# Half of the last batch's first product as seven block products, and two sums of w_in moved to GpSimd

## The chip, the cores and the metric

The kernel runs on one core of one Trainium2 chip. The metric is the device time in microseconds (us) of one execution; a run's time is the median of several executions. The engines are named as the profile names them: PE (TensorE: matmuls, with PEld for its weight loads), DVE (VectorE), ACT (ScalarE), POOL (GpSimd) and SP (SyncE, which here only issues DMAs). SBUF is the on-chip memory of all engines; PSUM holds the eight banks that PE writes its products to.

## What is computed

```python
scores  = scale * x @ state^T            # per batch (8) and head (8): 512 x 32, depth 64
xread   = softmax(scores) @ state        # 512 x 64
sread   = softmax(scale * state @ x^T) @ x   # 32 x 64
rows    = concat(xread, sread) per batch, heads side by side   # 8 x 544 rows of 512
h       = rows @ w_in                    # w_in 512 x 2048
g       = maximum(0.01 * h, h)           # leaky rectifier
out     = g @ w_out                      # w_out 2048 x 512, fp32
```

Two products of the feed-forward part make nearly all of the arithmetic. Operands are bf16, sums fp32.

## The kernel before

The kernel goes batch by batch through 512 token rows (`xread`); the 256 `sread` rows of all batches go through the feed-forward part together at the end.

For a batch, `xread @ w_in` is never formed from `xread`: `a.M` (256 x 2048, bf16, as [128, 2, 2048]) is state times w_in of that batch, made by `a_m` and copied out by `m_evict`, and `a.aT` (256 x 512, as [128, 2, 512]) holds the softmax weights. So **the first product** of a batch is `M^T aT`, depth 256 = two groups `g` of 128. `ff1(a, hT, j)` (L369) makes 128 of the 2048 rows of h: two matmuls of 512 columns into a PSUM tile `ph` (two buffers, used in turn), then the rectifier on ACT (L377) into `hT[:, j, :]`. The loop over `s` from 0 to 15 calls it with `j = s`.

**The second product** of a batch (`Batch`, `Fast`, L525 and L575) is done with seven block products where eight are usual. Its operands are A (from `hT`, split in two by token and two by depth) and B (from w_out). The products 1, 2, 6, 5, 7, 3, 4 accumulate in two PSUM banks `yq`: 1, 6, 7 and 4 in the first, 2, 5 and 3 in the second. Four sums of A, `su0` to `su3` (`sums`, L546, DVE, in halves: m 0 to 3 needs `hT` 0 to 7, m 4 to 7 the rest), and four of B (`tw`, made once) are the operands of products 6, 5, 7, 3 and 4. ACT saves the banks after 1, 6, 5 and 7 (L566), DVE joins them with the later ones (L569) into `yo`, and POOL adds one pair (L627).

A "unit" is one product at one m: two matmuls of 256 columns (L557). A batch has 56 units. 15 of them, of products 1 and 2, run in the batch's own loop; the other 41 run in the loop of the next batch, between its `ff1`. `PACE` says how many units each `s` runs; `fill(s)` runs them behind the `ff1` of that `s` (at s = 11 ahead of it). So in batch 7's loop PE takes product 2's rest and product 6 from s = 0 to 2, product 5 from 3, product 7 from 5, product 3 from 7 and product 4 from 9.

At the end of batch 6's loop and the start of batch 7's, DVE has, in this order: the softmax scaling of `a2` (`a_probs2`, L280, L282, L285), `su0`, `su1`, `su2` of batch 6 for m 0 to 3 (at s = 12), the same for m 4 to 7 with a join between, and `su3`. The order on each engine is the order in which the code calls it (`manual_schedule`); an engine takes its instructions strictly in turn, and each waits only for the semaphores of what it reads or overwrites. POOL's order in that stretch is: add of batch 5's second product (L627, in batch 6's loop), add of batch 6's (L627, in batch 7's loop).

**The sread rows** go through `FastIn` (L390) behind batch 7: also seven products, whose operands are four sums of w_in (`w_sum`, L411, 128x2048 bf16 each) and four small sums of x (L423). The sums of w_in are put into the four buffers of tag `xb` of `xpool`, which held x of batches 4 to 7. Sums 0 to 2 are made on DVE at s = 4 of batch 7, sum 3 and the x sums at s = 10. At s = 8 `a_sread` (L300) makes the last batch's `sread` with 16 small matmuls, which read the transpose of `a2`.

Of the kernel before, what the change touches and what calls it, by code (L numbers as in the profile page):

```python
# [9 lines left out]
P = 128  # L10
B, H, S, D = 8, 8, 512, 64
# [8 lines left out]
BF16 = mybir.dt.bfloat16  # L20
FP32 = mybir.dt.float32
AF = mybir.ActivationFunctionType
ALU = mybir.AluOpType
# [4 lines left out]
def kernel(  # L28
# [9 lines left out]
    nc = tc.nc  # L38
# [4 lines left out]
    att = ctx.enter_context(tc.tile_pool(name="att", bufs=2))  # L43
# [4 lines left out]
    psum = ctx.enter_context(tc.tile_pool(name="psum", bufs=2, space=bass.MemoryType.PSUM))  # L48
# [320 lines left out]
    def ff1(a, hT, j):  # L369
        ph = psum.tile([P, S], FP32, name="ph", tag="ph")  # L370
        for g in range(2):
            nc.tensor.matmul(  # L372
                ph[:], lhsT=a.M[:, g, P * j:P * (j + 1)],
                rhs=a.aT[:, g, :],
                start=(g == 0), stop=(g == 1),
            )
        nc.scalar.activation(out=hT[:, j, :], in_=ph[:], func=AF.Prelu, alpha=0.01)  # L377
# [12 lines left out]
    class FastIn:  # L390


        R = NK

        def __init__(self, hT):
            w = w_in_bf[:].rearrange("p (r k) (i f) -> p i r k f", r=2, i=2)
            self.W = {(i, r): w[:, i - 1, r - 1] for i in (1, 2) for r in (1, 2)}
            x = sr_t[:].rearrange("p (c b) (r k) n -> p r c k b n", r=2, c=2)
            self.X = {(r, c): x[:, r - 1, c - 1] for r in (1, 2) for c in (1, 2)}
            self.hT, self.S, self.T = hT, {}, {}  # L400
            self.bank, self.sv = [{}, {}], [None, None]

        def w_sum(self, n):
            W, S = self.W, self.S
            S[n] = xpool.tile([P, 2, DFF // 2], BF16, name=f"sw{n}", tag="xb")[:]
            u, v, op = (
                (W[2, 1], W[2, 2], ALU.subtract), (S[0], W[1, 1], ALU.subtract),
                (W[2, 1], W[1, 1], ALU.subtract), (W[1, 2], S.get(1), ALU.add),
            )[n]
            with nc.allow_low_precision(reason="operands of a product"):  # L410
                nc.vector.tensor_tensor(out=S[n], in0=u, in1=v, op=op)  # L411

        def x_sums(self):
            X, T = self.X, self.T
# [33 lines left out]
        def done(self, r, n, bank):  # L448
            R = self.R
            if n == 1:  # L450
                pool, tag, bufs = ((xpool, "xl", 1), (mpool, "M", 2))[r]
                self.sv[r] = pool.tile([P, 4, R * P], FP32, name=f"sf{r}", tag=tag, bufs=bufs)
            sv = {k: self.sv[r][:, i] for i, k in enumerate((1, 6, 5, 7))}
            flat = bank.rearrange("p q t -> p (q t)")

            def relu(i, c, src):
                nc.scalar.activation(
                    out=self.hT[:, 8 * i + R * r:8 * i + R * (r + 1), P * c:P * (c + 1)],
                    in_=src.rearrange("p (q t) -> p q t", q=R), func=AF.Prelu, alpha=0.01,
                )  # L460

            if n in (1, 6, 7):
                SCA(sv[n], flat)
            elif n == 5:
                VEC(sv[n], flat)
            if n in (2, 3):
                k = {2: 1, 3: 6}[n]
                nc.vector.tensor_tensor(out=sv[k], in0=flat, in1=sv[k], op=ALU.add)
                relu(0, n - 2, sv[k])
            elif n == 7:  # L470
                nc.gpsimd.tensor_tensor(out=sv[5], in0=sv[7], in1=sv[5], op=ALU.add)
            elif n == 4:
                relu(1, 1, sv[5])
                relu(1, 0, flat)

    class Y:
        pass
# [47 lines left out]
    class Fast:  # L525
# [9 lines left out]
        def sums(self, n, m0=0, m1=NM, eng=None):  # L535
            A, S = self.A, self.S
            if n not in S:
                pool, tag, bufs = self.homes[n]
                S[n] = pool.tile([P, NM, self.q], BF16, name=f"su{n}", tag=tag, bufs=bufs)
            u, v, op = (  # L540
                (A[2, 1], A[2, 2], ALU.subtract), (S[0], A[1, 1], ALU.subtract),
                (A[2, 1], A[1, 1], ALU.subtract), (A[1, 2], S.get(1), ALU.add),
            )[n]
            ms = slice(m0, m1)
            with nc.allow_low_precision(reason="operands of a product"):
                (eng or nc.vector).tensor_tensor(out=S[n][:, ms], in0=u[:, ms], in1=v[:, ms], op=op)  # L546
# [385 lines left out]
    for b in range(2, B):  # L932
        hT = hpool.tile([P, 16, S], BF16, name="hT", tag="hT")
        a = att_of[b]
        nxt = att_of[b + 1] if b + 1 < B else None
        now = Batch(b, hT)
        std = []
        if b == 2:
            std = [(i, 3) for i in range(2)] + [(i, jq) for i in range(2, NT) for jq in range(4)]

        def fill(s):
            n = (PACE2 if b == 2 else PACE)[s]
            left = min(n, len(before.units)) if before else 0
            if left:
                before.run(left)
            if n > left:
                now.run(n - left)

        for s in range(16):
            if s == 11:  # L950
                fill(s)
            ff1(a, hT, s)
            if s == 0:
                if b + 2 < B:
                    load_x(b + 2, nc.sync)
                    open_xb(b + 2)
                a_a2t(a)
                if before:
                    for n in (0, 1):
                        before.f.sums(n, 4, 8)  # L960
            elif s == 1:
                if nxt is not None:
                    a_scores(nxt)
                m_evict(a, 3, a_m(a, 3, "big"), SCA)
                if b == 2:
                    a_sread_rows([a0])
                if nxt is not None:
                    a_shift(nxt)
                if b + 2 < B:
                    for h in range(0, H, 2):  # L970
                        cast_x(b + 2, h, h + 2, POO)
                if before:
                    before.f.sums(2, 4, 8)
            elif s == 3:
                if before:
                    before.f.sums(3)
                if nxt is not None:
                    a_max2(nxt)
                if b == 2:
                    weights_sum(0)  # L980
                    weights_sum(2)
            elif s == 4:
                if b == 2:
                    state_t(1)
                elif b == 4:
                    sread_t(0, 4)
                elif b == 7:
                    sread_t(1, 3)
            elif s == 8:
                if nxt is None:  # L990
                    a_sread(a)
                if b == 2:
                    weights_sum(1)
                    weights_sum(3)
            elif s == 12:
                for n in range(3):
                    now.f.sums(n, 0, 4)
            if nxt is None:
                if s == 4:
                    fi = FastIn(None)  # L1000
                    for n in range(3):
                        fi.w_sum(n)
                elif s == 10:
                    fi.w_sum(3)
                    fi.x_sums()
            if s == (9 if b == 2 else 7) and b + 2 < B:
                a_open(att_of[b + 2], b + 2)
                a_xt_dma(att_of[b + 2])
            if nxt is not None:
                if s == 5:  # L1010
                    a_exp(nxt)
                elif s in (7, 8):
                    a_exp2(nxt, s - 7)
                    if s == 7:
                        a_probs(nxt)
                elif s == 11:
                    a_probs2(nxt)
                elif s in (12, 13):
                    SCA(nxt.M[:, s - 12, DM:2 * DM], pm1[:, s - 12, :])
            if std:  # L1020
                i, jq = std.pop(0)
                piece(1, h1, i, jq)
            elif s != 11:
                fill(s)
            if s == 10 and nxt is not None:
                a_sread_rows([a1, a2] if b == 2 else [a])
                pm0 = a_m(nxt, 0, "big")
                pm1 = a_m(nxt, 1, "sc")
                pm2 = a_m(nxt, 2, "ph")
                for g, copy in enumerate((VEC, SCA)):  # L1030
                    copy(nxt.M[:, g, 2 * DM:3 * DM], pm2[g][:])
                m_evict(nxt, 0, pm0, SCA)
        before = now
# [90 lines left out]
```

## Time and profile before

| | |
|---|---|
| median of 3 runs | 204.63 us (204.24 to 204.93) |
| the profiled execution | 204.49 us, of which its span (first to last instruction) is 202.7 |
| granted PE clock | 1.000 of full speed |
| ACT, 128x512 rectifier out of PSUM (L377) | 604 ns, 108 of them |
| ACT, 128x512 copy out of PSUM (L566) | 585 ns |
| DVE, 128x512 join out of PSUM (L569) | 685 ns |
| DVE, 128x1024 sum of bf16 (L546) | 700 ns |
| DVE, 128x2048 sum of bf16 (L411, at 161.56) | 1.22 us |
| POOL, 128x512 sum of fp32 (L627) | 1300 ns |
| batch 7's loop | 157.7 to 177.7 |

The profile has one row for an instruction, or for a few like ones in a row: start, length, engine, line, operation, what it writes <- what it reads, sizes as partitions x elements. A row's length holds the wait at the engine's ports, but not the wait for a semaphore, which shows as idle time before it; the bracket behind a row names what ended that idle time. Rows of one engine overlap by the fill and drain of its pipeline, so the spacing of starts, and not the length, is what a row costs in a full queue. The chain of waits goes back from the last instruction to what released it, and so on: what stands there sets the time.

### The profile page before, as it was taken

How to read it: one execution, taken by the hardware profiler on the slowest of the kernel's cores; microseconds unless marked ns; L12 is line 12 of the kernel's file. 1: busy time of each engine (PE TensorE's matmuls, PEld its weight loads, DVE VectorE, ACT ScalarE, POOL GpSimd, SP SyncE). 2: the span in 40 equal slices, each digit the busy share in tenths (PEclk: the TensorE clock that was granted, in tenths of full speed). 3: DMA queues.
4: the chain of work that ended last, by engine and by line, in shares of the span. 5: the costliest groups of instructions: out<-in, count | busy, mean ns of one | idle time of the engine just before them, and what ended most of it. 6: DMA issues, size and time to landing. Idle time of an engine off the chain costs nothing.

```text
span 202.7 us, 4755 instructions
## 1 busy us (share of the span) xinstructions
PE 197.0 (97%) x1964; PEld 126.0 (62%) x1964; DVE 151.4 (75%) x230; ACT 143.7 (71%) x265; POOL 39.7 (20%) x66
## 2 busy tenths in 40 slices
PE   7899999999999999999999999999999999999993
PEld 2543544444344567766776767766767677799882
DVE  1677679599799969976996699769968853686612
ACT  3458848589869796978697878788778856467710
POOL 8831002021005005200251040200020002004250
PEclk9999999999999999999999999999999999999999
DMA  6999996999477895537946795250017100410035
GB/s 189 223 207 277 229 298 113 141 303 245 53 175 214 114 275 109 103 125 253 118 29 181 240 127 105 103 159 5 0 57 198 27 0 32 178 55 0 3 89 170
DMA packets 39733, 27.99 MB, mean 138 GB/s; under 512 B 25312, under 2 KB 36704, under 8 KB 39712
## 3 DMA queue, kind: packets, MB, share of 16 engines
q1 hardware_dynamic: 34512, 20.88, 44.6%
q0 software_dynamic: 4912, 6.55, 15.8%
q10 hardware_dynamic: 288, 0.26, 0.6%
q8 instruction: 15, 0.25, 0.5%
q14 instruction: 6, 0.05, 0.1%
HBM read 17.30 MB, written 8.91 MB: 129 GB/s over the span
## 4 chain that ended last, share of the span: by engine, by line
PE 96%; DVE 1%; ACT 1%; issue 0%
PE yq L557 36%; PE ph L372 23%; PE py L487 10%; PE pm L351 4%; PE pyw L487 3%; PE pf L441 3%; PE yu L557 3%; PE pspin L132 3%; PE ph L804 2%; PE sc L206 1%; PE psn L318 1%; PE phw L383 1%; PE php L804 1%; DVE M L365 1%; ACT xT L666 1%; PE scn L695 0%
## 5 line engine op out<-in xcount | busy, mean ns | idle before, releaser
L377 ACT ACTIVATE hT<-ph 128x512 bf16<-128x512 f32 x108 | 63.5, 604 | 22.0 <-PE ph L372 21.4
L372 PE MATMUL ph<-aT,M 128*128 128x512 bf16 x216 | 62.3, 379 | 0.0
L557 PEld LDWEIGHTS <-su 128*128 128x128 bf16 x416 | 39.7, 98 | 14.5 <-DVE su L546 1.7
L557 PEld LDWEIGHTS <-hT 128*128 128x128 bf16 x288 | 27.7, 98 | 11.7 <-issue 1.1
L557 PE MATMUL yq<-tw_xf,su 128*128 128x256 bf16 x192 | 27.2, 273 | 0.0
L105 POOL CAST xb<-xl 128x512 bf16<-128x512 f32 (+1 forms) x21 | 14.4, 724 | 65.2 <-PE ph L372 40.6
L557 PE MATMUL yq<-w_out_bf,hT 128*128 128x256 bf16 x192 | 27.0, 273 | 0.0
L372 PEld LDWEIGHTS <-M 128*128 128x128 bf16 x216 | 21.0, 98 | 9.3 <-issue 0.8
L546 DVE TENSOR_TENSOR su<-hT 128x1024 bf16<-128x1024 bf16 x24 | 16.8, 700 | 10.5 <-ACT hT L377 10.5
L487 PE MATMUL py<-w_out_bf,hT 128*128 128x512 bf16 x96 | 24.2, 379 | 0.0
L487 PEld LDWEIGHTS <-hT 128*128 128x128 bf16 x128 | 12.1, 98 | 14.6 <-issue 0.9
L627 POOL TENSOR_TENSOR yo<-sv,sv 128x512 f32<-128x512 f32 x6 | 7.8, 1300 | 54.1 <-ACT sv L566 42.7
L569 DVE TENSOR_TENSOR yo<-yq,sv 128x512 f32<-128x512 f32 x17 | 11.6, 685 | 6.5 <-PE yq L557 6.5
L566 ACT COPY sv<-yq 128x512 f32<-128x512 f32 x24 | 13.9, 585 | 2.0 <-PE yq L557 1.4
L365 ACT CAST M<-pm 128x1024 bf16<-128x1024 f32 x13 | 13.2, 1014 | 0.9 <-PE pm L351 0.8
L557 PE MATMUL yq<-w_out_bf,su 128*128 128x256 bf16 x96 | 13.1, 273 | 0.0
L557 PE MATMUL yq<-tw_x,su 128*128 128x256 bf16 x96 | 13.1, 272 | 0.0
L557 PE MATMUL yq<-tw_x,hT 128*128 128x256 bf16 x88 | 12.1, 273 | 0.0
L274 ACT ACTIVATE e<-sc,mcols 128x512 bf16<-128x512 f32 x16 | 11.1, 696 | 0.0
L216 DVE TRANSPOSE_TENSOR_REDUCE mrow<-sc 128x32 f32<-128x1024 f32 x7 | 8.7, 1245 | 2.4 <-PE sc L206 2.4
L266 DVE TENSOR_REDUCE mcol<-sc 128x2 f32<-128x1024 f32 x8 | 9.7, 1215 | 0.0
L247 DVE STREAM_TRANSPOSE qb<-qh 128x1024 bf16<-128x1024 bf16 x7 | 8.7, 1245 | 0.2
(147 smaller groups left out, 271.3 us busy)
## 6 DMA issues: line engine op xcount, KB each, us to landing
xl<-in_x_dram SPq DMA_DIRECT2D x5, 1024.0 KB, 7.1
out_dram<-yo SPq DMA_DIRECT2D x10, 512.0 KB, 3.0
w_in_bf<-in_moe_w_in_dram POOLq DMA_DIRECT2D x4, 512.0 KB, 9.1
w_out_bf<-in_moe_w_out_dram POOLq DMA_DIRECT2D x4, 512.0 KB, 17.0
out_dram<-ysb SPq DMA_DIRECT2D x8, 256.0 KB, 5.1
xf<-in_x_dram SPq DMA_DIRECT2D x2, 512.0 KB, 4.8
x<-in_x_dram POOLq DMA_DIRECT2D x2, 512.0 KB, 13.8
xl<-in_x_dram POOLq DMA_DIRECT2D x1, 1024.0 KB, 19.8
```

The costliest lines, as they stand in the source:

```text
L105: copy(xs[b][:, :, h0:h1].rearrange("p t h d -> p h t d"), xl[b][:, h0:h1].rearrange("p h (t d) -> p h t d", t=NT),)
L216: nc.vector.tensor_reduce(out=m1[:], in_=flat.rearrange("p (c j) -> p c j", j=NS), axis=AX.X, op=ALU.max, apply_transpose=True,)
L266: nc.vector.tensor_reduce(out=m2[:], in_=a.sc[:], axis=AX.X, op=ALU.max, negate=True)
L274: nc.scalar.activation(out=a.e2[:, g], in_=a.sc[:, g, :], func=AF.Exp, bias=a.m2s[:, g:g + 1], scale=SCALE, accum_out=a.r2[:, g:g + 1],)
L365: copy(a.M[:, :, cols], pm[:])
L372: nc.tensor.matmul(ph[:], lhsT=a.M[:, g, P * j:P * (j + 1)], rhs=a.aT[:, g, :], start=(g == 0), stop=(g == 1),)
L377: nc.scalar.activation(out=hT[:, j, :], in_=ph[:], func=AF.Prelu, alpha=0.01)
L487: nc.tensor.matmul(y.py, lhsT=hT[:, j, P * i:P * (i + 1)], rhs=w_out_bf[:, j, :], start=(j == 0), stop=(j == 15),)
L546: (eng or nc.vector).tensor_tensor(out=S[n][:, ms], in0=u[:, ms], in1=v[:, ms], op=op)
L557: nc.tensor.matmul(bank[:, i, :], lhsT=lhs[:, m, P * i:P * (i + 1)], rhs=rhs[:, m, :], start=(first and m == 0 and (i == 0 or of is not No ...
L566: copy(t[:], bank)
L569: nc.vector.tensor_tensor(out=dst, in0=bank, in1=self.sv[n][:], op=ALU.add)
```

## The change

1. **`FastLast`.** In the last batch the rows j = 0 to 3 and 8 to 11 of the first product are made as seven block products over 2 x 2 blocks: i = 1, 2 (those two sets of rows), g = 1, 2 (depth), c = 1, 2 (tokens 0 to 255 and 256 to 511). It is done for two rows of each set at a time (r = 0, then r = 1): 14 products, each two matmuls of 256 columns, in two banks of tag `ph`. Eight sums (`lw` of M, 128x512, and `lx` of aT, 128x256, both bf16) are made first, on DVE at s = 1, ahead of `su3`. After product 1, 6 and 7 ACT copies the bank to SBUF, after 5 DVE does; after 2 and 3 DVE adds bank and copy; after 7 POOL adds two copies. Four rectifiers of 128x512 (as 128x2x256) for each r follow: `late` and `flush` put a rectifier that needs DVE's or POOL's sum behind the next copy on ACT.
2. **Order.** `ff1` runs for j = 4 to 7 at s = 0 to 3 and for 12 to 15 at s = 12 to 15. At s = 4 to 11 there are two products (one at s = 7 and 11), each followed by its share of the units of that s.
3. **Sums of w_in.** Sums 0 and 2 go to POOL, called at s = 1; sum 1 stays on DVE, at s = 8; sum 3 and the x sums come at s = 13.

```diff
-        def w_sum(self, n):
+        def w_sum(self, n, eng=nc.vector):
...
-                nc.vector.tensor_tensor(out=S[n], in0=u, in1=v, op=op)
+                eng.tensor_tensor(out=S[n], in0=u, in1=v, op=op)
...
+    class FastLast:
+        R, Q = 2, S // 2
+        ORDER = [(r, n) for r in range(2) for n in (1, 2, 6, 5, 7, 3, 4)]
...
+        def sums(self):
+            W, X, S, T = self.W, self.X, self.S, self.T
+            ws = att.tile([P, 4, 4 * P], BF16, name="lw", tag="sh", bufs=1)
+            xs = att.tile([P, 4, self.Q], BF16, name="lx", tag="e1", bufs=1)
...
+                for n in (0, 2, 1, 3):
...
+                        nc.vector.tensor_tensor(out=d, in0=u, in1=v, op=op)
+
+        def product(self):
+            r, n = self.todo.pop(0)
...
+            bank, sv = self.bank[2 if n in (2, 5, 3) else 1], self.sv
...
+            for q in range(R):
+                j = R * r + q
+                nc.tensor.matmul(
+                    bank[:, q, :], lhsT=lhs[:, P * j:P * (j + 1)], rhs=rhs,
+                    start=(n in (1, 2, 5) and q == 0), stop=True, skip_group_check=True,
+                )
...
+            if n in (1, 6, 7):
+                SCA(sv[n], flat)
+                self.flush()
+            elif n == 5:
+                VEC(sv[n], flat)
+            if n in (2, 3):
+                k = {2: 1, 3: 6}[n]
+                nc.vector.tensor_tensor(out=sv[k], in0=flat, in1=sv[k], op=ALU.add)
+                self.late.append((relu, 0, n - 2, sv[k]))
+            elif n == 7:
+                nc.gpsimd.tensor_tensor(out=sv[5], in0=sv[7], in1=sv[5], op=ALU.add)
+            elif n == 4:
+                relu(1, 0, flat)
+                self.flush()
+                self.late.append((relu, 1, 1, sv[5]))
...
         for s in range(16):
-            if s == 11:
+            fast = nxt is None and 4 <= s < 12
+            if fast:
+                n = 1 if s in (7, 11) else 2
+                k = PACE[s]
+                for i in range(n):
+                    fl.product()
+                    units((i + 1) * k // n - i * k // n)
+            elif s == 11:
                 fill(s)
-            ff1(a, hT, s)
+            if not fast:
+                ff1(a, hT, 4 + s if nxt is None and s < 4 else s)
...
             if nxt is None:
-                if s == 4:
+                if s == 1:
+                    fl = FastLast(a, hT)
+                    fl.sums()
                     fi = FastIn(None)
-                    for n in range(3):
-                        fi.w_sum(n)
-                elif s == 10:
+                    for n in (0, 2):
+                        fi.w_sum(n, nc.gpsimd)
+                elif s == 8:
+                    fi.w_sum(1)
+                elif s == 13:
+                    fl.flush()
                     fi.w_sum(3)
                     fi.x_sums()
```

More of the change, by code (lines that the diff above doesn't have):

```diff
@@ L474, in done, with __init__, relu, flush @@
                 relu(1, 0, flat)
+    class FastLast:
+        R, Q = 2, S // 2
+        ORDER = [(r, n) for r in range(2) for n in (1, 2, 6, 5, 7, 3, 4)]
+        def __init__(self, a, hT):
+            self.W = {(i, g): a.M[:, g - 1, P * 8 * (i - 1):P * (8 * (i - 1) + 4)] for i in (1, 2) for g in (1, 2)}
+            self.X = {(g, c): a.aT[:, g - 1, self.Q * (c - 1):self.Q * c] for g in (1, 2) for c in (1, 2)}
+            self.hT, self.S, self.T, self.sv = hT, {}, {}, {}
+            self.todo, self.late = list(self.ORDER), []
+        def sums(self):
+            W, X, S, T = self.W, self.X, self.S, self.T
+            ws = att.tile([P, 4, 4 * P], BF16, name="lw", tag="sh", bufs=1)
+            xs = att.tile([P, 4, self.Q], BF16, name="lx", tag="e1", bufs=1)
+            with nc.allow_low_precision(reason="operands of a product"):
+                for n in (0, 2, 1, 3):
+                    S[n], T[n] = ws[:, n], xs[:, n]
+                    for d, (u, v, op) in (
+                        (S[n], (
+                            (W[2, 1], W[2, 2], ALU.subtract), (S[0], W[1, 1], ALU.subtract),
+                            (W[2, 1], W[1, 1], ALU.subtract), (W[1, 2], S.get(1), ALU.add),
+                        )[n]),
+                        (T[n], (
+                            (X[1, 2], X[1, 1], ALU.subtract), (X[1, 1], T.get(2), ALU.subtract),
+                            (X[2, 2], X[1, 2], ALU.add), (T.get(1), X[2, 1], ALU.add),
+                        )[n]),
+                    ):
+                        nc.vector.tensor_tensor(out=d, in0=u, in1=v, op=op)
+        def product(self):
+            r, n = self.todo.pop(0)
+            R, Q = self.R, self.Q
+            if n == 1:
+                self.bank = {
+                    k: psum.tile([P, R, Q], FP32, name="pl", tag="ph")[:] for k in (1, 2)
+                }
+                homes = (("mrowb", 1), ("xT", 2)) if r == 0 else (("e2", 2), ("e2", 2), ("xT", 2))
+                ts = [
+                    att.tile([P, (2, 1)[t == "e2"], R * Q], FP32, name="ls", tag=t, bufs=c) for t, c in homes
+                ]
+                self.sv = dict(zip((1, 6, 5, 7), [t[:, i] for t in ts for i in range(t.shape[1])]))
+            bank, sv = self.bank[2 if n in (2, 5, 3) else 1], self.sv
+            lhs = {1: self.W[1, 1], 2: self.W[1, 2], 4: self.W[2, 2]}.get(n)
+            if lhs is None:
+                lhs = self.S[{3: 3, 5: 0, 6: 1, 7: 2}[n]]
+            rhs = {1: self.X[1, 1], 2: self.X[2, 1], 3: self.X[2, 2]}.get(n)
+            if rhs is None:
+                rhs = self.T[{4: 3, 5: 0, 6: 1, 7: 2}[n]]
+            for q in range(R):
[4 more added lines that the diff above has]
+                )
+            flat = bank.rearrange("p q t -> p (q t)")
+            def relu(i, c, src):
+                nc.scalar.activation(
+                    out=self.hT[:, 8 * i + R * r:8 * i + R * (r + 1), Q * c:Q * (c + 1)],
+                    in_=src.rearrange("p (q t) -> p q t", q=R), func=AF.Prelu, alpha=0.01,
+                )
+            if n in (1, 6, 7):
[13 more added lines that the diff above has]
+                self.late.append((relu, 1, 1, sv[5]))
+        def flush(self):
+            for f, *args in self.late:
+                f(*args)
+            self.late = []
@@ L941, in fill, with units @@
         def fill(s):
-            n = (PACE2 if b == 2 else PACE)[s]
+            units((PACE2 if b == 2 else PACE)[s])
+        def units(n):
             left = min(n, len(before.units)) if before else 0
@@ L1022 @@
                 piece(1, h1, i, jq)
-            elif s != 11:
+            elif s != 11 and not fast:
                 fill(s)
```

## The prediction

> **What bounds the kernel now.** I read the page first, then the chain of waits, then the timeline of the last two batches engine by engine. Page, parts 1 and 4:
>
> ```profile
> PE 197.0 (97%) x1964; PEld 126.0 (62%) x1964; DVE 151.4 (75%) x230; ACT 143.7 (71%) x265; POOL 39.7 (20%) x66
> ...
> PE 96%; DVE 1%; ACT 1%; issue 0%
> ```
>
> TensorE (PE) is the bound: whatever takes PE columns away saves time, and whatever makes PE wait costs its full length. The chain of waits where batch 7 begins (start, length, engine, tile, count):
>
> ```profile
> 157.23 0.66 PE yq L557 x6
> 159.31 0.98 PE yq L557 x8
> 160.72 0.87 PE yq L557 x8
> ```
>
> A matmul of 256 columns takes 0.87/8 = 0.109 us; the gaps from 160.29 to 160.72 are the two 512-column matmuls of one `ff1`, 0.43 us. PE streams without a hole. DVE and POOL in the middle of batch 6, from the timeline (start, length):
>
> ```profile
> 148.10 1.27 POOL L627 TENSOR_TENSOR yo<-sv,sv 128x512 f32<-128x512 f32 x1 [19.78 <-ACT sv L566]
> ...
> 148.70 1.22 DVE L248 TENSOR_TENSOR aT<-e,qb 128x1024 bf16<-128x1024 bf16 x1
> ...
> 153.26 0.16 DVE L280 TENSOR_SCALAR r<-r 128x2 f32<-128x2 f32 x1
> ...
> 153.46 0.17 DVE L282 RECIPROCAL qc<-r 128x2 f32<-128x2 f32 x1
> ...
> 153.66 0.61 DVE L285 TENSOR_SCALAR a<-e,qc 128x512 bf16<-128x512 bf16 x2
> ...
> 154.19 0.68 DVE L546 TENSOR_TENSOR su<-hT 128x1024 bf16<-128x1024 bf16 x1
> ...
> 154.91 0.69 DVE L546 TENSOR_TENSOR su<-su,hT 128x1024 bf16<-128x1024 bf16 x1
> ```
>
> The reader is to see that the L248 product took 1.22 us, where one of the same shape that met no Pool work (86.31) took 0.69, and that it ended 0.55 after Pool's add. A DVE instruction with two SBUF inputs stands still while a Pool instruction runs. DVE's SBUF `TENSOR_SCALAR` does too: at 45.62 one of 128x2 took 0.43 instead of 0.17, beside Pool casts. DVE instructions that read PSUM were not stretched. Pool's own prices, from the groups by shape:
>
> ```profile
> L627 POOL TENSOR_TENSOR yo<-sv,sv 128x512 f32<-128x512 f32 x6 | 7.8, 1300 | 54.1 <-ACT sv L566 42.7 <-issue 11.3
> ...
> L1076 POOL TENSOR_TENSOR yhs<-sv,sv 128x256 f32<-128x256 f32 x1 | 0.7, 723 | 2.3 <-ACT sv L566 2.3
> ```
>
> **The change, part by part.**
>
> *The product itself.* Eight `ff1` (16 matmuls of 512 columns, 3.45 us) become 14 products of two 256-column matmuls: 28 x 0.109 = 3.05. Saved 0.44 (in exact columns, four matmuls of 256). Weight loads rise by 12 of 0.098, beside matmuls of 0.109 each: hidden, as in the 1.05 us runs of eight L557 pairs, which hold the same ratio.
>
> *The two sums moved to Pool.* Their buffers are those of x of batches 4 and 5, last read by PE in those batches (near 109 and 130), and w_in is long there. So they don't wait for batch 7: Pool starts them as soon as it has done the add that ended at 149.37. Not shown: a Pool sum of 128x2048 bf16. The two rows above give (1.27 - 0.72)/256 = 2.1 ns an element, so 1.27 + 1536 x 0.0021 = **4.5 us**; the lower end is half per element for 2-byte data, 2.3. Pool's casts and copies take 0.8 ns an element, whether they read 4 or 2 bytes (L105 613 ns for 512 and 1042 for 1024, L80 and L84 196 and 209 ns for 16 and 32), so I take 4.5.
>
> Each then holds up DVE's SBUF work. L248, already waiting, goes first to 149.9; the first sum runs 149.9 to 154.4. L280 waits from 153.26 to 154.25, the second sum follows at 154.4 and runs to 158.9, and L285 waits until 158.75 instead of 153.66: 5.1 us late. (The stretched L248 gives the release as 0.14 before Pool's end.) Behind L285 on DVE stand all sums of batch 6's second product.
>
> The row shows one Pool instruction of 1.27 us holding DVE. [...]
>
> PE's waits follow:
> - *A.* `su1`, first half: before, it ended 1.94 us after L285 began; now 158.75 + 1.94 = 160.7. PE wants it at 159.31. **1.4**.
> - *B.* `su1`, second half: from the first half's start (160.0) DVE goes 0.61 + 0.61 + 0.72 + 0.69 (rows 154.91 to 159.23) to 162.63. PE has four units (0.87) and `ff1` (0.43) from 160.7, so wants it at 162.0. **0.65**.
> - *C.* Then DVE has a join (0.61), `su2` (0.60), the eight new sums, and `su3` (1.14). The 512-wide sums are spaced 0.35 (su at L546 of that shape, 188.08 to 188.43), the 256-wide 0.25 (L423): 4 x 0.60 = 2.4. `su3` ends near 167.3 and the first add out of PSUM (0.68, as L468) at 168.0. Product 5 overwrites that bank. PE, from 162.7: four units, `ff1`, four units, five single units and three products, 0.87 + 0.43 + 0.87 + 1.09 + 0.65 = 3.9, wants it at 166.6. **1.4**.
> - *D.* Second half of the rows. When product 4 of the first has ended, ACT has two rectifiers (0.54 each), a save (0.49) and the copy of product 1 (0.58), then DVE the add (0.60), the third w_in sum (1.14, still DVE's), a join (0.60) and the copy of product 5 (0.68): 5.3 with three hand-overs of 0.04 (the delay of ACT behind PE at 167.02 to 167.06). On PE there lie between them 13 units of 0.218 (2.83), five products (1.09) and the 16 small matmuls (0.47): 4.4. **0.9**, whatever Pool does.
>
> The other added work stands beside PE: six ACT copies (0.49 each) where ACT idled 0.2 to 0.8 before nearly every `ff1` of batch 7, two Pool adds (1.27) on a Pool that is done at 158.9, and four DVE adds and two copies out of PSUM where DVE idled 5.25 before 170.43; without that cover each is in C or D. The fourth w_in sum and the x sums move behind s = 13, 2.3 us of DVE work where it idled 2.11 before 177.94: 0, at most 0.2. SP issues the same DMAs in the same order; the transpose behind L285 comes 5 us later, near 159.5, and its reader is PE's small matmuls, past 168. Sum: 1.4 + 0.65 + 1.4 + 0.9 - 0.44 = +3.9. The profiled execution took 204.49 (span 202.7, 1.8 around it), close under the median of 204.63; so **208.4 us**.
>
> **The rivals.**
> 1. *Pool's sums don't hold DVE long* (2.3 us each, or a lock given up in between). L285 is then at most 1.2 late, and `su1`'s second half, which waited for ACT until 157.9, is in time. Left are D (0.9) and next to nothing of C (`su3` comes 2.4 later, the add ends at 164.65 where PE, by the chain, wants it at 164.63): +0.5, 205.0. For it: no row has a Pool instruction over 1.3 us beside DVE. Against it: every row of a Pool instruction beside a DVE sum shows the full wait.
> 2. *The gain survives* (the other side): as 1, and the line of D from ACT's rectifier to DVE's copy takes under 4.4 us. Price -0.44, 204.05. The point is the third w_in sum (1.14): were it done before that product 2's add could start, D would be gone. For it: DVE idles there. Against it: the sum is behind that add on DVE.
> 3. *Pool's sums are dearer*, 5 us or more each: a further 0.1 us comes twice into A, so 5.0 gives +4.9, 209.4. For it: their inputs are in two runs of 1024, where L627's are in one. Against it: L627's six lie between 1.26 and 1.47, the longest one itself beside a DVE sum.
>
> That the change doesn't do what it says: the two sums start a batch earlier than where they are written; that is in the forecast.
>
> **Numbers.** Forecast 67%, its own range 207.4 to 209.2 (a Pool sum of 4.1 to 4.9). Rival 1 17%, rival 2 5%, rival 3 11%. Range 204.9 to 209.5: it takes in rival 1 and the near end of 3. About 0.3% (0.6 us) is what a measurement here can tell from no change; faster by more takes rival 2 in part (0.04); within it lie the rest of 2 and most of 1 (0.13); slower is the rest (0.83).
>
> **What would show it.** Two POOL rows of L411 near 149.9 and 154.4 with 4.5 us each; L285 near 158.8; idle time of PE before `su1` units (A and B together 2.1), before `pl` products released by DVE (C 1.4, D 0.9); `ff1` gone from s = 4 to 11. Wrong would be: L411 on POOL near 2.3 us, DVE sums running during it, or no PE wait on `su1`.

## The result, and the profile after

| | before | after |
|---|---|---|
| median (range) | 204.57 us (204.24 to 204.93) | 207.68 us (207.43 to 208.73) |
| profiled execution, its span | 204.49, 202.7 | 207.43, 205.5 |
| granted PE clock | 1.000 | 1.000 |
| small matmuls of M of batch 7 to the first `pf` matmul | 26.82 us | 29.74 us |

Six runs of each give a ratio of 1.0161, with a 95% interval of [1.0136, 1.0185]: slower by 1.6%. The forecast was 208.4 us, +3.9 on the profiled execution; it became +2.94. The last row of the table is the measure used below, called the stretch. It is the time on the chain of waits from the first small matmul of `a_m` for batch 7 (151.11 before, 150.98 after) to the first matmul of the `sread` rows (177.93, 180.72). All of the change lies in it, and what differs between executions ahead of it is left out: +2.92.

Parts 1 and 4 of the page after:

```profile
PE 197.2 (96%) x1976; PEld 126.8 (62%) x1976; DVE 159.6 (78%) x242; ACT 147.0 (72%) x271; POOL 50.5 (25%) x70
...
PE 79%; DVE 7%; DMA 6%; SPq 2%; ACT 2%; issue 1%; POOL 1%; POOLq 0%; DVEq 0%
```

PE is busy as long as before (197.2 for 197.0) while the span is 2.8 longer: what came is idle time. Part 4 tells where to look: PE was 96% of the chain, and now DVE has 7% of it and ACT 2%. (From 18.7 to 40.6 this chain runs back over DMA and Pool's casts instead of PE, which takes most of PE's missing share; no time was lost there.) POOL in the timeline after, with start, length, line and tile:

```profile
147.97 1.27 POOL L713 TENSOR_TENSOR yo<-sv,sv 128x512 f32<-128x512 f32 x1 [19.78 <-ACT sv L652]
149.20 8.53 POOL L411 TENSOR_TENSOR sw<-w_in_bf 128x2048 bf16<-128x2048 bf16 x2
```

The two sums start right behind the add, a batch earlier than where they are written. The row holds both: 8.53 us, of which some 0.5 is the first one's wait for L248 on DVE (below, done at 149.79). That leaves **4.0 us for one sum**. DVE in the same view:

```profile
148.56 1.23 DVE L248 TENSOR_TENSOR aT<-e,qb 128x1024 bf16<-128x1024 bf16 x1
...
153.14 0.60 DVE L280 TENSOR_SCALAR r<-r 128x2 f32<-128x2 f32 x1
153.77 0.17 DVE L282 RECIPROCAL qc<-r 128x2 f32<-128x2 f32 x1
153.97 4.17 DVE L285 TENSOR_SCALAR a<-e,qc 128x512 bf16<-128x512 bf16 x2
158.06 0.68 DVE L632 TENSOR_TENSOR su<-hT 128x1024 bf16<-128x1024 bf16 x1
...
165.80 0.68 DVE L548 TENSOR_TENSOR ls<-pl,ls 128x512 f32<-128x512 f32 x1
...
171.02 0.69 DVE L548 TENSOR_TENSOR ls<-pl,ls 128x512 f32<-128x512 f32 x1 [2.00 <-ACT ls L542]
171.63 1.36 DVE L411 TENSOR_TENSOR sw<-sw,w_in_bf 128x2048 bf16<-128x2048 bf16 x1
172.92 0.68 DVE L655 TENSOR_TENSOR yo<-yq,sv 128x512 f32<-128x512 f32 x1
173.52 0.68 DVE L545 COPY ls<-pl 128x512 f32<-128x512 f32 x1
```

The 128x2 `TENSOR_SCALAR` at 153.14 takes 0.60 for 0.16: it stands until the first Pool sum lets go, at about 153.7. L285 is issued at 153.97 and its row lasts 4.17 for 0.61: it stands until the second sum lets go. So `su0` (L632; L546 before) begins at 158.06, where it began at 154.19. Not all of DVE's work is held: beside the two sums the reciprocal at 153.77 took its usual 0.17, and the joins out of PSUM at 149.71 and 152.53 their usual 0.68 and 0.69. PE, with what it waited for in brackets:

```profile
159.53 1.05 PE L643 MATMUL yq<-tw_xf,su 128*128 128x256 bf16 x8 [0.34 <-ACT hT L377]
161.45 1.05 PE L643 MATMUL yq<-tw_xf,su 128*128 128x256 bf16 x8 [0.45 <-DVE su L632]
166.53 0.38 PE L529 MATMUL pl<-lx,lw 128*128 128x256 bf16 x2 [0.98 <-DVE ls L548]
174.25 0.38 PE L529 MATMUL pl<-aT,lw 128*128 128x256 bf16 x2 [0.84 <-DVE ls L545]
```

These are four waits at the four places that the prediction called A to D. (In the first the profile names ACT's `hT`. That rectifier and DVE's sum both end at 159.47. Before, the same matmuls started at 159.24, ahead of the end of this rectifier at 159.60, so they don't need it: it is DVE's sum that they wait for.) The chain of waits after shows A and B as one run of DVE work, and D at its end:

```profile
153.97 4.17 DVE a L285 x2
158.14 0.61 DVE su L632
158.78 1.91 DVE su L632 x3
160.70 0.70 DVE su L632
161.45 1.05 PE yq L643 x8
...
172.92 0.68 DVE yo L655
173.59 0.61 DVE ls L545
```

Before, the same stretch of the chain was PE alone. (At C the chain names ACT's copy of product 6, which ended at 165.74, ahead of DVE's add at 165.80. The add doesn't need it: in run 2 below it began at 164.25, before that copy began at 164.73. It came late because it stood behind `su3` on DVE.)

### The profile page after: what moved, and what is told of

Its sections match the earlier page's. It is cut to its first block, busy times and chain, and to the rows that moved or that the text cites. A ratio compares the mean times of both kernels' runs of the same rounds, so it can differ in the third digit from the quotient of the medians.

```text
span 205.5 us, 4807 instructions
## 1 busy us (share of the span) xinstructions
PE 197.2 (96%) x1976; PEld 126.8 (62%) x1976; DVE 159.6 (78%) x242; ACT 147.0 (72%) x271; POOL 50.5 (25%) x70
## 4 chain that ended last, share of the span: by engine, by line
PE 79%; DVE 7%; DMA 6%; SPq 2%; ACT 2%; issue 1%; POOL 1%; POOLq 0%; DVEq 0%
PE yq L643 32%; PE ph L372 19%; PE py L573 7%; PE pm L351 4%; DMA stf<-in_state_dram 3%; PE pf L441 3%; PE yu L643 3%; DMA xT<-xb 3%; PE pspin L132 2%; DVE a L285 2%; SPq L170 2%; DVE su L632 2%; PE ph L890 1%; PE psn L318 1%; PE pl L529 1%
## 5 line engine op out<-in xcount | busy, mean ns | idle before, releaser
L377 ACT ACTIVATE hT<-ph 128x512 bf16<-128x512 f32 x100 | 58.9, 604 | 16.4 <-PE ph L372 15.9
L372 PE MATMUL ph<-aT,M 128*128 128x512 bf16 x200 | 57.7, 379 | 0.0
L372 PEld LDWEIGHTS <-M 128*128 128x128 bf16 x200 | 19.3, 98 | 8.9 <-issue 1.0
L632 DVE TENSOR_TENSOR su<-hT 128x1024 bf16<-128x1024 bf16 x24 | 16.8, 701 | 6.8 <-ACT hT L377 6.7
```

The source lines that it names most:

```text
L372: nc.tensor.matmul(ph[:], lhsT=a.M[:, g, P * j:P * (j + 1)], rhs=a.aT[:, g, :], start=(g == 0), stop=(g == 1),)
```

## Experiments

The theory: Pool's two sums hold up DVE's SBUF work one instruction at a time, which makes A and B, and through them C; D is a separate line from ACT's rectifiers over DVE's third sum of w_in to DVE's copy, and comes with the seven products whatever Pool does. The main rivals: the added copies and sums of the seven products cost the time by themselves, with Pool beside the point; or ACT is the bound in this stretch.

**1. The Pool sums alone**, put into the kernel before (`w_sum` takes the engine as in the change).

```diff
-                    for n in range(3):
-                        fi.w_sum(n)
+                    for n in (0, 2):
+                        fi.w_sum(n, nc.gpsimd)
+                    fi.w_sum(1)
```

> The kernel before, with only sums 0 and 2 of w_in given to Pool (first product as before, eight ff1). [...] Rival (Pool's sums are harmless and the new product's own DVE and ACT work makes the loss): DVE loses 2.3 us of work, PE waits for nothing, 204.5, no change.

With 4.0 us a sum, the theory put a wait of 0.4 us at A and one of 0.6 at B, +1.0 and 205.5 in all.

Measured: 205.72 us against 204.70 in the same session, 1.0048 [1.0026, 1.0070]; the stretch became 1.04 longer. DVE, then PE, in its timeline:

```profile
154.26 4.17 DVE L285 TENSOR_SCALAR a<-e,qc 128x512 bf16<-128x512 bf16 x2
```

```profile
159.81 1.05 PE L557 MATMUL yq<-tw_xf,su 128*128 128x256 bf16 x8 [0.34 <-ACT hT L377]
161.74 1.05 PE L557 MATMUL yq<-tw_xf,su 128*128 128x256 bf16 x8 [0.67 <-DVE su L546]
```

The same two waits, without a single one of the first product's block products. A and B are Pool's doing.

**2. The change without Pool's sums.** DVE makes sums 0 and 2 behind `su2` at s = 12 of batches 5 and 6; sum 1 stays on DVE at s = 8.

```diff
             elif s == 12:
                 for n in range(3):
                     now.f.sums(n, 0, 4)
+                if b == 5:
+                    fi = FastIn(None)
+                    fi.w_sum(0)
+                elif b == 6:
+                    fi.w_sum(2)
...
-                    fi = FastIn(None)
-                    for n in (0, 2):
-                        fi.w_sum(n, nc.gpsimd)
```

> The changed kernel, with sums 0 and 2 of w_in on DVE, in idle time behind its su2 at s = 12 of batches 5 and 6; sum 1 stays at s = 8 of batch 7. Theory: A and B are gone (no wait of PE for su1), C falls from 1.2 to 0.2 or less, D stays near 1.0; +0.6 us over the kernel before, 205.1. Rival (the new product's own work makes the loss): 207 or more, since DVE has 2.3 us more to do than in the changed kernel.

Measured: 205.54 us, 1.0040 [1.0019, 1.0060]; stretch +0.78. Of PE's four waits one is left, D:

```profile
172.72 0.38 PE L529 MATMUL pl<-aT,lw 128*128 128x256 bf16 x2 [0.85 <-DVE ls L545]
```

C went together with A and B, though all eight `lw`/`lx` sums were still there.

**3. One Pool sum per batch**: as the change, but Pool's sum 0 is called in batch 6's loop, so that it runs 20 us earlier.

```diff
+                if b == 6:
+                    fi = FastIn(None)
+                    fi.w_sum(0, nc.gpsimd)
...
-                    fi = FastIn(None)
-                    for n in (0, 2):
-                        fi.w_sum(n, nc.gpsimd)
+                    fi.w_sum(2, nc.gpsimd)
```

> The changed kernel, with sum 0 on Pool called in batch 6 (it runs behind Pool's add in batch 5's second half, near 128.7) and sum 2 on Pool as in the changed kernel (149.7 to 153.7). The same work on Pool, but one sum at a time. Theory: each sum ends when DVE reaches L280 and L285, which wait 0.5 at most; su1 is in time, A and B are gone, C is 0.2 or less, D stays: +0.6 us, 205.1. Rival (what costs is that Pool does the sums at all, by slowing PE's or ACT's reads or DVE's every instruction): most of the +2.9 stays, 207.

Measured: 205.72 us, 1.0051 [1.0020, 1.0082]; stretch +0.77. POOL in its timeline:

```profile
128.42 4.52 POOL L411 TENSOR_TENSOR sw<-w_in_bf 128x2048 bf16<-128x2048 bf16 x1
...
149.47 4.52 POOL L411 TENSOR_TENSOR sw<-w_in_bf 128x2048 bf16<-128x2048 bf16 x1
```

Two separate rows of 4.52, each with the same 0.5 us of waiting for L248, give the 4.0 us again; and 8.53 for two less 4.52 for one is 4.01 for the second. With one Pool sum in the way, L280 still stood (0.60), but L285 ran in 0.62. A, B and C were gone and D stayed (0.84 at 172.38): it is the second sum in a row that costs, since L285 then has to wait a whole one.

**4. The Pool sums in halves**: each of the two as two instructions of 128x1024.

```diff
-                eng.tensor_tensor(out=S[n], in0=u, in1=v, op=op)
+                for k in range(2) if eng is nc.gpsimd else (slice(0, 2),):
+                    eng.tensor_tensor(out=S[n][:, k], in0=u[:, k], in1=v[:, k], op=op)
```

> The changed kernel, each of Pool's two sums cut into two instructions of 128x1024 (2.05 us each). [...] Rival (DVE goes first as soon as it gets a gap): both of L285 and the su sums go at 155.6, A and B are gone, 206.5.

If the two take turns by instruction, L280 goes behind the second half and L285's two instructions behind the third and the fourth, and the time stays at the change's: 207.5.

Measured: 207.61 us against 204.51, 1.0154 [1.0139, 1.0169]; stretch +3.00, so 0.1 more than the change. POOL, then DVE, in its timeline:

```profile
149.65 8.87 POOL L412 TENSOR_TENSOR sw<-w_in_bf 128x1024 bf16<-128x1024 bf16 x4
```

```profile
153.59 0.74 DVE L280 TENSOR_SCALAR r<-r 128x2 f32<-128x2 f32 x1
...
154.57 4.10 DVE L285 TENSOR_SCALAR a<-e,qc 128x512 bf16<-128x512 bf16 x2
158.60 0.68 DVE L633 TENSOR_TENSOR su<-hT 128x1024 bf16<-128x1024 bf16 x1
```

The halves didn't let DVE in earlier. L280 (0.74 for 0.16) got in at the boundary between two halves, as in the change between the two sums (0.60). L285 is a row of two instructions, and each now met a half of its own: the row lasts 4.10 where it lasted 4.17 beside one whole sum. DVE's instructions that write `a`, in stretches of half a microsecond (start:end, length, busy time of DVE with count, PEclk, DMA share, GB/s), show where the first ends and the second begins, which is between 156.0 and 157.0:

```profile
155.50:156.00 0.50, 0.50 (x1) 1.00 0.68 270
156.00:156.50 0.50, 0.50 (x2) 1.00 0.00 0
...
157.00:157.50 0.50, 0.50 (x1) 1.00 0.00 0
```

Here DVE and Pool alternate by instruction, so what is lost is Pool's work, in halves (L285's 4.10) as in whole sums (4.17).

**5. The seven products alone**: sums 0 to 2 on DVE at s = 4, their place before the change.

```diff
+                elif s == 4:
                     fi = FastIn(None)
-                    for n in (0, 2):
-                        fi.w_sum(n, nc.gpsimd)
-                elif s == 8:
-                    fi.w_sum(1)
+                    for n in range(3):
+                        fi.w_sum(n)
```

> The changed kernel, with sums 0, 1 and 2 of w_in on DVE at s = 4 of batch 7, where they were before. Theory: no A, no B, C 0.2 or less, D gone (sum 1 is early); but the three sums (3.5 us) stand on DVE between the add of product 2 and the copy of product 5, so PE waits 2.8 at the first half's product 3: +2.6 us, 207.1. Rival (the new product gains its 0.44 once Pool is left alone): 204.1.

Measured: 209.14 us, 1.0203 [1.0159, 1.0248]; stretch +4.35, 1.7 more than expected. DVE, then PE, in its timeline:

```profile
164.24 1.22 DVE L411 TENSOR_TENSOR sw<-w_in_bf 128x2048 bf16<-128x2048 bf16 x1
165.49 1.22 DVE L411 TENSOR_TENSOR sw<-sw,w_in_bf 128x2048 bf16<-128x2048 bf16 x1
166.63 1.22 DVE L411 TENSOR_TENSOR sw<-w_in_bf 128x2048 bf16<-128x2048 bf16 x1
167.77 0.68 DVE L545 COPY ls<-pl 128x512 f32<-128x512 f32 x1
```

```profile
168.50 0.38 PE L529 MATMUL pl<-aT,lw 128*128 128x256 bf16 x2 [2.66 <-DVE ls L545]
```

The wait itself is as expected: three sums stand ahead of the copy out of PSUM that PE needs. The rest is in the granted clock, from the stretches of half a microsecond (start:end, length, busy time of PE, PEld, DVE, ACT and POOL with counts, PEclk, DMA share, GB/s):

```profile
169.00:169.50 0.50, 0.50 (x7) 0.44 (x6) 0.50 (x1) 0.00 (x0) 0.50 (x1) 1.00 0.00 0
169.50:170.00 0.50, 0.50 (x5) 0.38 (x3) 0.18 (x1) 0.43 (x1) 0.35 (x1) 0.57 0.17 33
170.00:170.50 0.50, 0.50 (x5) 0.33 (x3) 0.00 (x0) 0.50 (x2) 0.00 (x0) 0.50 0.00 0
...
173.00:173.50 0.50, 0.50 (x19) 0.49 (x17) 0.17 (x1) 0.00 (x0) 0.00 (x0) 1.00 0.00 0
```

One microsecond after PE had begun again, the clock fell to half for 3.5 us (169.5 to 173.0), which loses about 3.5 / 2 = 1.75 us. All four runs show a mean clock of 0.989 to 0.992; the kernel before ran at 0.996 to 1.000.

**6. The same with PE kept busy**: 11 matmuls of 512 columns on zeros, whose result nobody reads, stand in the wait.

```diff
+                    if (s, i) == (6, 1):
+                        spin(11, "big")
                     fl.product()
```

> The kernel with seven products alone (three sums on DVE at s = 4, PE idle 2.7 us at the first half's product 3), with eleven matmuls of 512 columns on zeros put into that wait (their result isn't used): 2.4 us more PE work. Theory (the idle time itself set the granted clock to a half for 3.5 us): the clock stays at 1, the product still starts near 168.5, and the time falls by 1.6 us, from 209.1 to 207.5. Rival (the half clock comes from somewhere else, such as the load): it stays, and the time is 209 or more.

Measured: 207.20 us against 204.51, 1.0133 [1.0120, 1.0146]; stretch +2.69. PE in its timeline, and PEclk (third number from the end) in one stretch of 2 us:

```profile
165.49 2.54 PE L132 MATMUL pspin<-idle 128*128 128x512 bf16 x11
...
168.31 0.38 PE L529 MATMUL pl<-aT,lw 128*128 128x256 bf16 x2 [0.28 <-DVE ls L545]
```

```profile
170.00:172.00 2.00, 2.00 (x33) 1.84 (x31) 0.50 (x1) 2.00 (x5) 0.89 (x1) 1.00 0.00 0
```

PE has more to do than in run 5, and the stretch is 1.7 us shorter. The 1.7 us were the clock, and the idle time brought them. In the change no single wait is over 1.0, and the clock of its profiled execution stayed at 1.00.

**7. All sums of w_in in idle time of DVE**: as run 2, and sum 1 goes to s = 9 of batch 6.

```diff
-                elif s == 8:
-                    fi.w_sum(1)
...
+            if b == 6 and s == 9:
+                fi.w_sum(1)
```

> As the second kernel (sums 0 and 2 on DVE behind su2 at s = 12 of batches 5 and 6), and sum 1 taken out of batch 7 too: on DVE at s = 9 of batch 6, where it idles 1.45. Theory (D is the third sum standing between an add and a copy): D falls from 1.0 to nothing, C stays at 0.1, 0.1 stays for ACT's copy behind its other work; with the 0.44 saved the time is 0.2 under the kernel before, 204.4. Rival (D comes from ACT's six added copies, not from the sum): PE still waits 0.5 or more at the second half's product 3, 204.9 or more.

Measured: 204.52 us against 204.51, 0.9995 [0.9986, 1.0005]; stretch -0.13. D is gone: no wait of PE is long enough for a bracket. Two of the moved sums on DVE:

```profile
149.93 1.21 DVE L411 TENSOR_TENSOR sw<-sw,w_in_bf 128x2048 bf16<-128x2048 bf16 x1
...
155.61 1.22 DVE L411 TENSOR_TENSOR sw<-w_in_bf 128x2048 bf16<-128x2048 bf16 x1
```

They stand where DVE had idled, and PE doesn't notice. ACT as the bound of this stretch is out as well: all its added copies are still in this kernel. But the 0.44 us of removed columns isn't earned either. PE's starts show gaps of 0.12 (ahead of 170.05) and 0.10 (170.81) between the second half's products and 0.03 (164.00) in the first half, each ahead of a product that goes into a bank which ACT or DVE has just read.

**8. and 9. Two tries at the rest.** In one, `su3` moves behind the seven products' first joins, to s = 5; in the other, no rectifier stands between ACT's copy of product 1 and the next.

```diff
# 8, on top of 7
             elif s == 3:
-                if before:
+                if before and nxt is not None:
                     before.f.sums(3)
...
+                elif s == 5:
+                    before.f.sums(3)
# 9, on top of 7
             if n in (1, 6, 7):
                 SCA(sv[n], flat)
-                self.flush()
+                if n != 1:
+                    self.flush()
```

> As the kernel with all three sums in idle time, and su3 of batch 6 moved behind the copy of product 5 (called at s = 5 of batch 7 and not at s = 3), so that the first add out of PSUM doesn't stand behind it. Theory: C is gone as well, PE waits 0.1 in all, 0.3 under the kernel before, 204.3. Rival (C was never DVE's queue, or su3 is now late for product 3 of batch 6): 204.6 or more.

> As the kernel with all three sums in idle time, with the rectifier that waits for Pool's add moved on ACT from behind the second half's copy of product 1 to behind its copy of product 6. Theory (what is left of the 0.44 goes into ACT's copies being late for products 7 and 3 of the second half, 0.12 and 0.10): the copy of product 6 comes 0.5 earlier, both gaps close, PE's stretch from the small M matmuls at 151 to the first product of the sread rows takes 26.5 us (26.82 in the kernel before, 26.69 with the sums in idle time), 204.3 in all. Rival (those gaps come from elsewhere): 26.7, 204.5.

Measured: 204.59 us against 204.51 (1.0001 [0.9990, 1.0011]) and 204.42 against 204.42 (0.9996 [0.9984, 1.0008]); the stretch was 0.07 and 0.08 shorter than before. Neither gained. In run 9 the copy of product 6 began only 0.06 earlier, since ACT now reached the casts of `psr` first and these waited for PE. What is left is a row of short hand-overs between PE and the engine that empties its bank; which of them could be saved was not settled.

## Why the prediction was right

The sign, the four places and the mechanism were right; the size was one microsecond too large.

| step | predicted | after, from PE's starts | on its own |
|---|---|---|---|
| A, `su1` first half | 1.4 | 0.42 | A and B together 1.04 (run 1) |
| B, `su1` second half | 0.65 | 0.61 | |
| C, product 5 waits for DVE's add | 1.4 | 1.17 | 0 without A and B (runs 2, 3) |
| D, product 3 waits for DVE's copy | 0.9 | 1.15 | 0.85 of wait (run 2) |
| removed columns | -0.44 | -0.44 | 0.13 gained in all (run 7) |
| sum | +3.9 | +2.9 | |

(A: the first `su1` unit started at 159.53 for 159.24 before, and this execution was 0.13 early. B: 161.45 for 160.55, less the 0.29 by which the first half was later. C: by the prediction's 3.91 of PE work, product 5 would have started at 161.45 + 3.91 = 165.36. D: by the same prices 6.57 us of work lie between product 5's start and 174.25, which is 7.72 later.)

- **The term that was mis-sized is A**, by the price of a Pool sum. The prediction went from 256 and 512 elements at 2.1 ns each to 4.5 us for 2048; the rows show 4.0, which is (4.0 - 1.27) / 1536 = 1.8 ns an element. Two sums in a row bring the 0.5 us in twice, 1.0 us, all of it in A, the first wait: A fell from 1.4 to 0.42. The other prices worked out beside it, 2.3 us from half the time per element and over 5 us, were both wrong. The prediction's own range, 207.4 to 209.2, holds the median, but it was given for a sum of 4.1 to 4.9 us, and the measured price lies just under that.
- **That Pool holds DVE for the whole instruction** was the step that decided between the forecast and the first rival. The kernel before shows it for a Pool instruction of 1.27 us (L248 took 1.22 for 0.69); that it goes on for one three times as long was the author's estimate, and so were the 5.1 us by which the prediction had L285 late. The change bears the step out: L285's row lasts 4.17 us for 0.61 beside sums of 4.0, and `su0` behind it began 3.9 us later than before. Run 1 shows the same 4.17 without the seven products. Run 4 adds what happens between instructions: they take turns.
- **C** is a consequence of A and B and not a cost of its own. DVE's eight sums and the add fit when `su1` is in time (runs 2 and 3); they are only late when DVE starts them late. C came 0.23 under the forecast and D 0.25 over it; that the two cancel in the sum is luck.
- **D, whatever Pool does**: right, as runs 2 and 3 show it alone. Its 1.15 is 0.25 more than predicted: the third w_in sum took 1.36 instead of 1.22, beside Pool's add from 170.64 to 171.91, and ACT could begin only when the row of product 4 had ended, at 168.88, where the prediction counted PE's time from the start of its next row, at 168.71.
- **The second rival** (the gain survives) had named the point: the third w_in sum out of D's line. Run 7 did that and took A to C away as well, and D closed; but the price of -0.44 came to -0.13. The prediction counted the ACT copies and rectifiers as covered where ACT idled. They are, for ACT; the short waits of PE for each hand-over, 0.25 in run 7, were not counted, and the last 0.06 stays open.

## What to carry to other kernels

Work that is moved to Pool starts when Pool's queue reaches it and its inputs and buffers allow, which may be a batch earlier than where it is written (here at 149.20, as the add of 147.97 ended). Look for what DVE does in SBUF at that time, and count each Pool instruction's full length (4.0 us here, of which L285 stood 3.6) as a possible wait for the next DVE one; the rows of the trace show which of DVE's instructions are held. Here two of Pool's sums in a row cost 1.04 us (run 1) and one at a time nothing that the stretch shows (+0.77 in run 3, +0.78 in run 2 without Pool sums): the slack takes up the first and none is left for the second. A saving in matmul columns (here 0.44 of 204, of which run 7 kept 0.13) pays in full only where the copies that it adds leave no hand-over on PE's path, and the slot of any other long DVE operation near them has to be chosen for that.

## What the runs showed of the hardware that was not expected

- **The clock after a short wait.** In run 5 PE idled 2.66 us; a microsecond after it resumed the granted clock was halved for 3.5 us, and that cost 1.7 us on top of the wait. With PE kept busy (run 6) it did not happen, and in the change's profiled execution, with waits of up to 1.0 us, it did not happen either. One of the ten runs of experiment 3, which has no trace, also had a mean clock of 0.992, so this wait need not be the only cause. From how much idle time on it happens was not tried.
- **Turns between DVE and Pool.** A `TENSOR_SCALAR` of 128x2, 0.16 us by itself, took 0.60 in the change and 0.74 in run 4 beside the rest of a Pool sum or half, while the `RECIPROCAL` of 128x2 behind it was not held (0.17 in both). Two halves of a sum, met one after the other, held L285 as long (4.10) as one whole sum (4.17).
